# r and k of the tenth chunk on turned by a DMA in 2-byte halves, and softmax work ahead of weight conversion

## The chip, the cores and the metric

One NeuronCore of a Trainium2 chip runs the whole kernel. The metric is the device time of one launch in microseconds (us), the median of several runs. The engines named below are PE (TensorE: matmuls and transposes, with PEld for its weight loads), DVE (VectorE), ACT (ScalarE), POOL (GpSimd) and SP (SyncE, which here only issues DMAs). Each engine works through its own instructions strictly in the order in which the program puts them; semaphores hold an instruction until what it needs is there.

## The reference

A linear attention with a decaying state (RWKV-5) feeds a feed-forward block with a SoLU and a layer norm:

```
for t in range(S):                       # B=4, H=8, S=768, D=48
    cur = einsum('bhd,bhe->bhde', u * k[t], v[t])
    y[t] = einsum('bhd,bhde->bhe', r[t], state + cur)
    state = w * state + einsum('bhd,bhe->bhde', k[t], v[t])
x = y as (3072, 384)
h = x @ w_in                             # 384 -> 1024
solu = h * softmax(h)
ln = (solu - mean) / sqrt(var + 1e-6) * g_ln
out = ln @ w_out                         # 1024 -> 384
```

The weights of the feed-forward block arrive as 8-byte floats and are turned into 4-byte ones on the chip. All other data is float32.

## The kernel before

The 3072 rows are cut into 24 **units** of 128 rows (4 batches times 6 chunks of 128 steps), numbered 0 to 23 with the batch as the fast index. A diff calls a unit's chunk by that number too: "the tenth chunk on" are units 9 to 23.

For one unit the attention does the following. `turn_r` and `turn_k` (L692, L699) transpose r and k on PE, four 128x128 transposes each through PSUM (`tr_ps`, `tk_ps`), so that the head dimension lies on the partitions; DVE multiplies the turned r by a table of inverse powers of w (`fore`) while it copies it out of PSUM (`rT`, L697), and ACT copies the turned k out (`kT`, L707). k was multiplied by its powers of w before (`decay_k`, POOL, `kp`). `weigh` and `sum_own` make each row's own term, `diagonal` (ACT, L690) lays it on a diagonal matrix `AT`. `scores` (PE, `at`, L720) makes the products of k and r, which DVE copies into `AT` behind a mask (L723). `finish` (PE) makes y (`y_ps`, L748) and the state's update (`kv_ps`, L766, not for the last chunk of a batch), ACT copies y out as `xT` (L760), DVE and POOL update the state.

The feed-forward part: `ffn_in` (PE, `h_ps`, L783) with an exponential on ACT behind it (L786), `unit` (L789) with a reciprocal and the product `solu` on DVE (L793, L795), a shift and a square on ACT (L797, L798) and two small POOL instructions for the deviation (L799, L801). `h_ps` has one buffer: the next `ffn_in` can start only when L795 has read it. `halve_ln` (L807) has ACT split the 4-byte words of `solu` into two planes of 2-byte halves (L814) and SP issue a transposing DMA of these (L816). `join_ln` (L819) has DVE weave the turned halves into words again, `lnT` (L822). `ffn_out` (PE, `o_ps`, L830) multiplies by w_out, ACT scales by the deviation (L833), SP stores.

The main loop (L841) is a software pipeline written out by hand; what it calls is the order on every engine. In **iteration i** stand, among others: loads for units i+5 and i+3; `turn_r` and `turn_k` of unit i+2; `decay_k` and `weigh` of unit i+3; `scores` of unit i+1 and `finish` of unit i; `ffn_in` and `unit` of unit j = i-2; `halve_ln` of unit i-5, `join_ln` of i-6, `ffn_out` of unit l = i-7. So iterations 2 to 6 have `ffn_in` but no `ffn_out` ("early"), 7 to 23 have all, 24 to 30 drain. Iterations -2 to 5 also convert the 14 weight pieces, w_in's six first: `convert_a` (ACT, L518), `convert_b` (DVE, L531 and L533), `convert_c` (POOL, L541) and for w_out's eight also `convert_d` (DVE, L548). Iterations 7 to 20 load each piece again for a range check (`check_words`, L559, L561).

The tiles for raw weights, for `halves` and for `turned` come from one ring of six buffers (tag "raw"). A new tile takes the buffer whose last reader stands furthest back among the free ones in program order, and its first writer waits for that reader.

Of the kernel before, what the change touches and what calls it, by code (L numbers as in the profile page):

```python
# [399 lines left out]
def direct_path(  # L400
# [26 lines left out]
    nc = tc.nc  # L427
# [10 lines left out]
    LA, LO = 2, 5  # L438
# [174 lines left out]

    kdec = const.tile([128, HP, 128], F32, name="kdec")

    def turn_table():
        kd_ps = psM.tile([128, HP, 128], F32, tag="m", name="kd_ps")
        for a in range(HP):
            nc.tensor.transpose(kd_ps[:, a, :], back[:, a, :], ident)
        nc.scalar.copy(out=kdec, in_=kd_ps)  # L620
# [70 lines left out]

    def turn_r(i):  # L692
        rT = live.setdefault(i, {})["rT"] = apool.tile([128, HP, T], F32, name="rT", bufs=3)
        ps = psM.tile([128, HP, T], F32, tag="m", name="tr_ps")
        for a in range(HP):
            nc.tensor.transpose(ps[:, a, :], pair(rpads[i % NLD], a), ident)  # L696
        nc.vector.tensor_mul(rT, ps, fore)  # L697

    def turn_k(i):  # L699
        X = live[i]  # L700
        X["kT"] = apool.tile([128, HP, T], F32, name="kT")
        ps = psM.tile([128, HP, T], F32, tag="m", name="tk_ps")

        for a in range(HP):
            nc.tensor.transpose(ps[:, a, :], pair(X["kp"] if i > 0 else kpads[0], a), ident)  # L705
        if i > 0:
            nc.scalar.copy(out=X["kT"], in_=ps)  # L707
        else:
            nc.vector.tensor_mul(X["kT"], ps, back)
# [79 lines left out]
    def unit(i):  # L789
        X = live[i]  # L790
        st = small.tile([128, 8], F32, name="st", bufs=LO + 3)
        rs, tot, ss, var, rstd = (st[:, n : n + 1] for n in range(5))
        nc.vector.reciprocal(out=rs, in_=sums[:, i : i + 1])  # L793
        solu = X["solu"] = fpool.tile([128, dff], F32, name="solu", bufs=LO + 2)
        nc.vector.scalar_tensor_tensor(out=solu, in0=X["h"], scalar=rs, in1=X["e"],  # L795
                                       op0=ALU.mult, op1=ALU.mult, accum_out=tot)
        nc.scalar.activation(out=solu, in_=solu, func=ACT.Identity, scale=-float(dff), bias=tot)  # L797
        nc.scalar.activation(out=X["e"], in_=solu, func=ACT.Square, accum_out=ss)  # L798
# [7 lines left out]

    def halve_ln(i):  # L807
        X = live[i]

        halves, turned = (wpool.tile([128, dff // 2, 2], U32, tag="raw", name=name, bufs=6)  # L810
                          .bitcast(U16).rearrange("p n o -> p (n o)")
                          for name in ("halves", "turned"))
        halves = halves.rearrange("p (o n) -> p o n", o=2)
        nc.scalar.copy(out=halves, in_=X["solu"].bitcast(U16).rearrange("p (n o) -> p o n", o=2))  # L814
        X["turned"] = turned.rearrange("p (o f t) -> p o f t", o=2, f=KF)
        nc.sync.dma_start(out=X["turned"].rearrange("p o f t -> p (o f) t"),  # L816
                          in_=halves.rearrange("p o n -> p (o n)"), transpose=True)

    def join_ln(i):  # L819
        X = live[i]  # L820
        lnT = X["lnT"] = fpool.tile([128, KF, 128], F32, name="lnT")
        nc.vector.tensor_copy(out=lnT.bitcast(U16).rearrange("p f (t o) -> p o f t", o=2),  # L822
                              in_=X["turned"])
# [17 lines left out]
    for i in range(-2, N + LA + LO):  # L841
# [10 lines left out]
        before, now = now, [todo.pop(0) for _ in range(conversions.get(i, 0))]  # L852
        if i == -2:
            turn_r(0)
            turn_k(0)
            turn_table()
# [8 lines left out]
        if i == LA:  # L865
            nc.vector.tensor_single_scalar(out=minus_g, in_=g_sb, scalar=-1.0, op=ALU.mult)
# [19 lines left out]
        for p in now[: 1 if i >= LA else 2]:  # L886
# [4 lines left out]
        if 1 <= i and i + 3 < N:  # L891
            weigh(i + 3, nc.gpsimd)
        if i == 10:
# [7 lines left out]
        if 0 <= l + 1 < N:  # L901
            join_ln(l + 1)
        if not early:
# [9 lines left out]
        elif i >= LA:  # L913
            unit(j)
# [6 lines left out]
        if i == 1:  # L921
            sum_own(3)
        if early and 0 <= i:
            diagonal(i + 2)
        for p in now[1:] if i >= LA else []:
            convert_b(p)
            convert_c(p)
# [43 lines left out]
```

## Time and profile before

| | |
|---|---|
| time, median of 3 runs (lowest to highest) | 370.79 us (370.27 to 370.82) |
| the profiled execution's own time | 370.75 us |
| its span, first to last instruction | 368.8 us |
| granted PE clock, mean | 0.999 |
| busy share of the span: PE, PEld, DVE, ACT, POOL | 95%, 58%, 50%, 64%, 40% |
| first `ffn_in` of an early iteration | 27.27 us |
| first `ffn_in` of an iteration with `ffn_out` (7) | 77.50 us |
| last matmul group starts | 358.37 us |

A row of a timeline reads: start in us, length in us, engine, line of the kernel, operation, what is written <- what is read, shapes, how many instructions were merged, and in brackets how long the engine stood idle before it and whose end released it. PE matmuls are pipelined and their ends modelled, so starts are compared rather than lengths. The profiled execution's own time lies 2.0 us above its span and 0.04 us under the median, so a change of the span is taken as a change of the time.

### The profile page before, as it was taken

What the parts mean: (1) busy time and instruction counts of PE and PEld (TensorE: products, weight loads), DVE (VectorE), ACT (ScalarE), POOL (GpSimd) and SP (SyncE); (2) the same over time, 40 slices, a digit from 0 to 9 for tenths busy, and PEclk for the clock granted to TensorE, in tenths of its full rate; (3) what the DMA queues carried; (4) which work ended last, traced back from release to release, by engine and by line L of the source; (5) the groups of instructions that cost most, each with busy time, mean ns of one, the idle gap of its engine ahead of it and who ended that gap; (6) DMA issues with size and microseconds to landing.
All of it is one profiled execution on the core that took longest, in us unless ns stands there. A gap on an engine that the chain in (4) does not pass through costs nothing.

```text
span 368.8 us, 8576 instructions
## 1 busy us (share of the span) xinstructions
PE 349.7 (95%) x3527; PEld 214.2 (58%) x3527; DVE 185.9 (50%) x333; ACT 234.2 (64%) x455; POOL 145.8 (40%) x181
## 2 busy tenths in 40 slices
PE   3789999889999999999999999999999999999994
PEld 2475566557566565565664675665655565555552
DVE  7797886784563853653553534535524323133220
ACT  3865879869756676577477477666765644556410
POOL 3889766744551442533624615515420000222000
PEclk9999999999999999999999999999999999999999
DMA  8999993784964854954836746545333033312731
GB/s 172 257 234 250 212 207 47 121 161 93 186 143 87 174 116 89 181 111 93 173 78 123 148 87 140 127 83 121 88 59 78 24 79 58 74 46 59 156 78 52
DMA packets 133533, 44.88 MB, mean 122 GB/s; under 512 B 126701, under 2 KB 129902, under 8 KB 133486
## 3 DMA queue, kind: packets, MB, share of 16 engines
q1 hardware_dynamic: 133342, 44.06, 57.4%
q8 instruction: 29, 0.48, 0.6%
q10 hardware_dynamic: 144, 0.20, 0.3%
q14 instruction: 18, 0.15, 0.1%
HBM read 26.94 MB, written 4.72 MB: 86 GB/s over the span
## 4 chain that ended last, share of the span: by engine, by line
PE 78%; DVE 10%; POOL 5%; issue 3%; ACT 2%; DMA 1%; POOLq 0%; DVEq 0%; ACTq 0%
PE o_ps L830 34%; PE h_ps L783 27%; PE y_ps L748 8%; PE at L720 4%; PE tr_ps L696 2%; DVE solu L795 2%; PE tk_ps L705 2%; DVE w_out_sb L548 2%; PE kv_ps L766 1%; DVE ma L533 1%; DVE rT L697 1%; POOL ma L541 1%; DVE AT L723 1%; ACT solu L797 1%; ACT e L798 1%
## 5 line engine op out<-in xcount | busy, mean ns | idle before, releaser
L783 PE MATMUL h_ps<-w_in_sb,xT 128*128 128x512 f32 x288 | 128.4, 595 | 5.0 <-DVE solu L795 3.9
L830 PE MATMUL o_ps<-w_out_sb,lnT 128*128 128x384 f32 x384 | 127.2, 486 | 0.0
L830 PEld LDWEIGHTS o_ps<-w_out_sb,lnT 128*128 128x128 f32 x384 | 72.9, 190 | 54.7 <-issue 9.1
L783 PEld LDWEIGHTS h_ps<-w_in_sb,xT 128*128 128x128 f32 x288 | 52.9, 190 | 64.1 <-issue 59.0
L799 POOL TENSOR_SCALAR st<-st 128x1 f32<-128x1 f32 x24 | 9.0, 375 | 149.4 <-ACT e L798 149.4
L690 ACT ACTIVATE AT<-ident,own 128x128 f32<-128x128 f32 x192 | 58.5, 390 | 5.4 <-DVE own L684 5.4
L723 DVE COPY_PREDICATED AT<-later,at 128x512 f32<-128x512 uint32 x48 | 32.8, 736 | 53.6 <-PE at L720 53.6
L786 ACT ACTIVATE e<-h_ps 128x1024 f32<-128x1024 f32 x24 | 24.6, 1023 | 44.4 <-PE h_ps L783 44.4
L822 DVE COPY lnT<-turned 128x2048 uint16<-128x2048 uint16 x24 | 37.2, 1550 | 20.6 <-DMA turned<-halves 13.3
L814 ACT COPY halves<-solu 128x2048 uint16<-128x2048 uint16 x24 | 45.5, 1894 | 0.0
L793 DVE RECIPROCAL st<-sums 128x1 f32<-128x1 f32 x24 | 3.8, 160 | 64.5 <-ACT e L786 64.5
L797 ACT ACTIVATE solu<-solu,st 128x1024 f32<-128x1024 f32 x24 | 27.4, 1142 | 13.0 <-DVE solu L795 13.0
L673 POOL TENSOR_TENSOR kp<-kpad,kdec 128x512 f32<-128x512 f32 x24 | 30.6, 1277 | 7.4 <-ACT kdec L620 6.3
L795 DVE SCALAR_TENSOR_TENSOR solu<-h_ps,st,e 128x1024 f32<-128x1024 f32 x24 | 30.8, 1284 | 2.1
L679 POOL TENSOR_TENSOR rku<-kpad,u_bc 128x384 f32<-128x384 f32 x23 | 30.8, 1341 | 0.0
L760 ACT COPY xT<-y_ps 128x384 f32<-128x384 f32 x24 | 11.4, 475 | 30.2 <-PE y_ps L748 30.2
L680 POOL TENSOR_TENSOR rku<-rku,rpad 128x384 f32<-128x384 f32 x23 | 27.8, 1209 | 1.8
L720 PE MATMUL at<-rT,kT 48*64 48x128 f32 (+1 forms) x768 | 27.9, 265 | 0.0
L720 PEld LDWEIGHTS at<-rT,kT 48*64 48x64 f32 x768 | 21.8, 139 | 10.4 <-issue 9.7
L773 POOL TENSOR_TENSOR state<-state,pw 64x192 f32<-64x192 f32 x32 | 17.0, 530 | 26.3 <-DVE state L772 25.1
L748 PE MATMUL y_ps<-AT,vt 128*32 128x128 f32 x768 | 26.3, 279 | 0.0
L798 ACT ACTIVATE e<-solu 128x1024 f32<-128x1024 f32 x24 | 25.4, 1057 | 0.8
(77 smaller groups left out, 315.6 us busy)
## 6 DMA issues: line engine op xcount, KB each, us to landing
raw<-in_moe_w_in_dram SPq DMA_DIRECT2D x12, 512.0 KB, 5.8
raw<-in_moe_w_out_dram SPq DMA_DIRECT2D x16, 384.0 KB, 4.8
kpad<-in_k_dram SPq DMA_DIRECT2D x24, 192.0 KB, 4.5
rpad<-in_r_dram SPq DMA_DIRECT2D x24, 192.0 KB, 4.6
vt<-in_v_dram SPq DMA_DIRECT2D x24, 192.0 KB, 4.5
out_dram<-o SPq DMA_DIRECT2D x24, 192.0 KB, 2.1
turned<-halves SPq DMA_TRANSPOSE x24, 4.3
u_bc<-in_u_dram ACTq DMA_DIRECT2D x1, 192.0 KB, 3.6
```

Source lines behind the costliest of these rows:

```text
L673: nc.gpsimd.tensor_mul(X["kp"].rearrange("p h d -> p (h d)"), kpads[i % NLD].rearrange("p h d -> p (h d)"), kdec.rearrange("p a d -> p (a ...
L679: engine.tensor_mul(rku, kpads[i % NLD][:, :, 0:D], u_bc)
L690: nc.scalar.activation(out=AT[:, h, :], in_=ident, func=ACT.Copy, scale=X["own"][:, h])
L720: nc.tensor.matmul(pss[q][ts(c, P), a, c * P :], X["kT"][rows, a, ts(c, P)], X["rT"][rows, a, c * P :], start=True, stop=True)
L723: nc.vector.copy_predicated(A4[:, :, q, :], later.to_broadcast([128, HP, T]), pss[q])
L748: nc.tensor.matmul(y_ps[32 * g : 32 * g + 32, j, :], lhsT, rhs, start=(g not in opened), stop=stop, skip_group_check=True)
L783: nc.tensor.matmul(h_ps[:, ts(n, NX)], X["xT"][:, j, :], w_in_sb[:, j, ts(n, NX)], start=(j == 0), stop=(j == KD - 1))
L795: nc.vector.scalar_tensor_tensor(out=solu, in0=X["h"], scalar=rs, in1=X["e"], op0=ALU.mult, op1=ALU.mult, accum_out=tot)
L797: nc.scalar.activation(out=solu, in_=solu, func=ACT.Identity, scale=-float(dff), bias=tot)
L814: nc.scalar.copy(out=halves, in_=X["solu"].bitcast(U16).rearrange("p (n o) -> p o n", o=2))
L822: nc.vector.tensor_copy(out=lnT.bitcast(U16).rearrange("p f (t o) -> p o f t", o=2), in_=X["turned"])
L830: nc.tensor.matmul(o_ps, X["lnT"][:, f, :], w_out_sb[:, f, :], start=(f == 0), stop=(f == KF - 1))
```

## The change

Units 0 to 8 are turned on PE as before. From unit 9 on (`FIRST`), r is multiplied by its powers before it is turned (`decay_r`, POOL, with the table `rdec`, which is turned once on PE in iteration 1). `halve_rk` in iteration i splits unit i+3: ACT splits `kp` (L861), DVE splits `rp` (L862), both into one tile of 2048 halves per partition, and SP issues one transposing DMA of it. `join_rk` in iteration i+1 has DVE weave the turned halves into the tile `rk` (two halves `rT` and `kT`; three buffers, where `kT` had two). The eight PE transposes, the DVE product and the ACT copy of these units are gone.

In the early iterations `unit` now stands right behind `turn_r`, ahead of the conversions; `convert_b` goes to the end of the iteration for both pieces, `convert_c` to the start of the next, `convert_d` to that one's end. `minus_g` is made in iteration 1. In all iterations the two small POOL instructions of a unit (`deviation`) stand one iteration later. `solu` has five buffers, not seven.

```diff
-    LA, LO = 2, 5
+    LA, LO, FIRST = 2, 5, 9
...
+    def decay_r(i):
+        X = live[i]
+        X["rp"] = apool.tile([128, H, P], F32, name="rp")
+        nc.gpsimd.tensor_mul(X["rp"].rearrange("p h d -> p (h d)"),
+                             rpads[i % NLD].rearrange("p h d -> p (h d)"),
+                             rdec.rearrange("p a d -> p (a d)"))
...
-        nc.gpsimd.tensor_scalar(out=var, in0=ss, scalar1=1.0 / dff, scalar2=1e-6 * dff ** 2,
-                                op0=ALU.mult, op1=ALU.add)
-        nc.gpsimd.tensor_tensor(out=rstd, in0=var, in1=neg_half, op=ALU.pow)
-        X["rstd"] = rstd
+        X["st"] = ss, var, rstd
+
+    def deviation(i):
+        ss, var, rstd = live[i]["st"]
+        live[i]["rstd"] = rstd
...
+    def turn(both):
+        turned = halves()
+        nc.sync.dma_start(out=turned.rearrange("p (n t) -> p n t", t=128), in_=both,
+                          transpose=True)
+        return turned.rearrange("p (o n t) -> p o n t", o=2, t=128)
+
+    def join(words, turned):
+        nc.vector.tensor_copy(out=words.bitcast(U16).rearrange("p n (t o) -> p o n t", o=2),
+                              in_=turned)
...
+    def halve_rk(i):
+        if i < FIRST:
+            return
+        X = live[i]
+        both = halves()
+        parts = both.rearrange("p (o e n) -> p o e n", o=2, e=2)
+        nc.scalar.copy(out=parts[:, :, 1], in_=split(X["kp"].rearrange("p h d -> p (h d)")))
+        nc.vector.tensor_copy(out=parts[:, :, 0], in_=split(X["rp"].rearrange("p h d -> p (h d)")))
+        X["turned"] = turn(both)
+
+    def join_rk(i):
+        X = factors(i)
+        join(X["rk"].rearrange("p e a t -> p (e a) t"), X["turned"])
...
+        for p in before:
+            if pieces[p][2] is not None:
+                convert_c(p)
...
-        for p in before:
-            convert_d(p)
-        if i >= LA:
-            for p in now[:1]:
-                convert_b(p)
         if -2 < i and i + 2 < N:
-            turn_r(i + 2)
+            if i + 2 < FIRST:
+                turn_r(i + 2)
+            else:
+                join_rk(i + 2)
+            if early and i >= LA:
+                unit(j)
             if i < 0 or i >= LA:
                 sum_own(i + 2)
-            turn_k(i + 2)
+            if i + 2 < FIRST:
+                turn_k(i + 2)
...
+            if i + 3 >= FIRST:
+                decay_r(i + 3)
...
+        if 0 <= j - 1 < N:
+            deviation(j - 1)
...
+        if i + 3 < N:
+            halve_rk(i + 3)
...
-        elif i >= LA:
-            unit(j)
...
+            turn_table(fore, rdec)
...
+        if i >= LA:
+            for p in before:
+                convert_d(p)
+            for p in now:
+                convert_b(p)
```

On PE, between iterations 8 and 9, stood the end of unit 8 (`y_ps`, `kv_ps`), the turning of unit 11 and the feed-forward products of units 7 and 2:

```order
L748 MATMUL y_ps_1407<-rT_1062,state0_164 32x128 x12
L748 MATMUL y_ps_1407<-AT_1167,vt2_96 32x128 x16
L766 MATMUL kv_ps_1438<-vt2_96,kp_947 32x48 x16
L696 MATMUL tr_ps_1463<-ident_151,rpad1_85 128x128 x4
L705 MATMUL tk_ps_1472<-ident_151,kp_1335 128x128 x4
L783 MATMUL h_ps_1494<-w_in_sb_104,xT_1293 128x512 x6
L830 MATMUL o_ps_1520<-w_out_sb_105,lnT_1349 128x384 x8
```

The same place on PE in the changed kernel:

```order
L762 MATMUL y_ps_1400<-rk_1057,state0_164 32x128 x12
L762 MATMUL y_ps_1400<-AT_1168,vt2_96 32x128 x16
L780 MATMUL kv_ps_1431<-vt2_96,kp_945 32x48 x16
L797 MATMUL h_ps_1484<-w_in_sb_104,xT_1291 128x512 x6
L874 MATMUL o_ps_1508<-w_out_sb_105,lnT_1339 128x384 x8
```

The two groups of four transposes are gone, and `ffn_in` follows `finish` directly.

On ACT, in iterations 6 and 7, stood the exponential of unit 4, the split of unit 1, the shift and square of unit 4, unit 6's `xT`, the diagonal of unit 8, and then iteration 7 up to its exponential (unit 5):

```order
L786 ACTIVATE e_1058,sums_206<-h_ps_1051 128x1024 [waits PE_49]
L707 COPY kT_1071<-tk_ps_1072 128x512 [waits PE_49]
L814 COPY halves_1083<-solu_701 128x2048
L797 ACTIVATE solu_1091<-solu_1091,st_1089 128x1024 [waits DVE_49]
L798 ACTIVATE e_1058,st_1089<-solu_1091 128x1024 [waits Activation_49]
L760 COPY xT_1144<-y_ps_1115 128x384 [waits PE_49]
L690 ACTIVATE AT_1167<-ident_151,own_1069 128x128 x8
L707 COPY kT_1188<-tk_ps_1189 128x512 [waits PE_49]
L814 COPY halves_1202<-solu_821 128x2048
L786 ACTIVATE e_1215,sums_206<-h_ps_1208 128x1024 [waits PE_49]
```

The same stretch on ACT in the changed kernel (`halves_1093` is the first tile of r and k, unit 9; `halves_1203` the second, unit 10; DMAHW5 is the semaphore of unit 9's transposing DMA):

```order
L800 ACTIVATE e_1053,sums_207<-h_ps_1046 128x1024 [waits PE_49]
L811 ACTIVATE solu_1066<-solu_1066,st_1064 128x1024 [waits DVE_49]
L812 ACTIVATE e_1053,st_1064<-solu_1066 128x1024 [waits Activation_49]
L721 COPY rk_1057<-tk_ps_1072 128x512 [waits PE_49]
L847 COPY halves_1087<-solu_681 128x2048
L861 COPY halves_1093<-kp_1078 128x2x512 [waits Pool_49]
L774 COPY xT_1145<-y_ps_1116 128x384 [waits PE_49]
L699 ACTIVATE AT_1168<-ident_151,own_1070 128x128 [waits DVE_49]
L699 ACTIVATE AT_1168<-ident_151,own_1070 128x128 x7
L847 COPY halves_1197<-solu_800 128x2048 [waits DMAHW0_49,DVE_49]
L861 COPY halves_1203<-kp_1186 128x2x512 [waits DVE_49,DMAHW5_49,Activation_49,Pool_49]
L800 ACTIVATE e_1215,sums_207<-h_ps_1208 128x1024 [waits PE_49]
```

The shift and square moved ahead of unit 1's split; the splits of k are new, and the one of unit 10 waits for unit 9's DMA, with iteration 7's exponential behind it.

On DVE, at the start of iteration 7, stood unit 9's product, its own term, `lnT` of unit 1 and the product `solu` of unit 5:

```order
L697 TENSOR_TENSOR rT_1179<-tr_ps_1180,tab_172 128x512 [waits PE_49]
L684 TENSOR_REDUCE own_1186<-rku_1080 128x8 [waits Pool_49]
L822 COPY lnT_1206<-turned_1084 128x2x1024 [waits DMAHW4_49]
L793 RECIPROCAL st_1226<-sums_206 128x1 [waits Activation_49]
L795 SCALAR_TENSOR_TENSOR solu_1228,st_1226<-h_ps_1208,st_1226,e_1215 128x1024 [waits DVE_49,PE_49]
```

The same place on DVE in the changed kernel:

```order
L841 COPY rk_1182<-halves_1096 128x2x1024 [waits DMAHW5_49]
L693 TENSOR_REDUCE own_1184<-rku_1082 128x8 [waits Pool_49]
L841 COPY lnT_1201<-halves_1089 128x2x1024 [waits DMAHW4_49]
L862 COPY halves_1203<-rp_1188 128x2x512 [waits DVE_49,Activation_49,Pool_49]
L807 RECIPROCAL st_1226<-sums_207 128x1 [waits Activation_49]
L809 SCALAR_TENSOR_TENSOR solu_1228,st_1226<-h_ps_1208,st_1226,e_1215 128x1024 [waits DVE_49,PE_49]
```

Where a product waited for PE stands a copy that waits for unit 9's DMA, and one more copy stands ahead of `solu`.

More of the change, by code (lines that the diff above doesn't have):

```diff
@@ L815, in halve_ln @@
-        X["turned"] = turned.rearrange("p (o f t) -> p o f t", o=2, f=KF)
-        nc.sync.dma_start(out=X["turned"].rearrange("p o f t -> p (o f) t"),
-                          in_=halves.rearrange("p o n -> p (o n)"), transpose=True)
+        both = halves()
+        nc.scalar.copy(out=both.rearrange("p (o n) -> p o n", o=2), in_=split(X["solu"]))
+        X["turned"] = turn(both)
     def join_ln(i):
         X = live[i]
-        lnT = X["lnT"] = fpool.tile([128, KF, 128], F32, name="lnT")
@@ L855, in direct_path @@
             turn_k(0)
[L856 removed]
+            turn_table(back, kdec)
             weigh(0, nc.vector)
```

44 lines of the change are left out of this document (24 added, 20 removed).

## The prediction

> **What bounds the kernel now.** I read the page first, then the chain of waits, then the timeline of PE where the chain leaves PE. The page's first part gives busy times and shares, its fourth the chain that ended last:
>
> ```profile
> span 368.8 us, 8576 instructions
> ...
> PE 349.7 (95%) x3527; PEld 214.2 (58%) x3527; DVE 185.9 (50%) x333; ACT 234.2 (64%) x455; POOL 145.8 (40%) x181
> ...
> PE 78%; DVE 10%; POOL 5%; issue 3%; ACT 2%; DMA 1%; POOLq 0%; DVEq 0%; ACTq 0%
> ```
>
> PE is busy 95% and carries 78% of the chain. An average hides stages, so the chain in order of time (start, length, what) comes next, around the start of iteration 8 and at two later places:
>
> ```profile
> 91.10 0.59 PE tr_ps L696 x4
> 91.69 0.44 PE tk_ps L705 x4
> 92.13 5.15 PE h_ps L783 x12
> ...
> 264.47 5.15 PE h_ps L783 x12
> ...
> 278.50 5.15 PE h_ps L783 x12
> ...
> 291.50 5.35 PE h_ps L783 x12
> ```
>
> From 77.5 us on the chain never leaves PE: (264.47-92.13)/12 = 14.36 us for each of twelve iterations, with the eight transposes of one unit inside. What is taken from PE there shortens the run, as long as nothing else then arrives late. Before 77.5 us it is otherwise. This is the timeline of PE, `ffn_in` of iterations 4, 5, 6, 7 and 8, and the transposes ahead of iteration 7's:
>
> ```profile
> 45.81 5.39 PE L783 MATMUL h_ps<-w_in_sb,xT 128*128 128x512 f32 x12 [0.70 <-DVE solu L795]
> 55.26 5.39 PE L783 MATMUL h_ps<-w_in_sb,xT 128*128 128x512 f32 x12 [0.16 <-PE kv_ps L766]
> 65.89 5.39 PE L783 MATMUL h_ps<-w_in_sb,xT 128*128 128x512 f32 x12 [1.33 <-DVE solu L795]
> 75.11 0.66 PE L696 MATMUL tr_ps<-ident,rpad 128*128 128x128 f32 x4
> 77.50 5.42 PE L783 MATMUL h_ps<-w_in_sb,xT 128*128 128x512 f32 x12 [1.30 <-DVE solu L795]
> 91.96 5.32 PE L783 MATMUL h_ps<-w_in_sb,xT 128*128 128x512 f32 x12
> ```
>
> PE has 9.22 us of work in an early iteration (65.89 to 75.11, no wait inside), but waits up to 1.33 us more for `solu`, which must free the only `h_ps`.
>
> **Part 1: the transposes from iteration 8's on.** Iterations 7 to 21 lose their eight transposes; 7's and 8's are counted in part 2, which leaves 13. The chain would price eight at 0.59+0.44 = 1.03 us, but `h_ps` is 0.20 us longer where none stand ahead of it (5.35 against 5.15). The cleaner price is from start to start on PE's timeline, with the transposes between (iteration 21) and without (22):
>
> ```profile
> 276.42 1.06 PE L748 MATMUL y_ps<-AT,vt 128*32 128x128 f32 x32
> ...
> 283.48 5.32 PE L830 MATMUL o_ps<-w_out_sb,lnT 128*128 128x384 f32 x16
> ...
> 290.44 1.06 PE L748 MATMUL y_ps<-AT,vt 128*32 128x128 f32 x32
> ...
> 296.68 5.32 PE L830 MATMUL o_ps<-w_out_sb,lnT 128*128 128x384 f32 x16
> ```
>
> 7.06 against 6.24: 0.82 us, of which 0.11 is a longer `h_ps`. Most iterations have `kv_ps` in between as well, and I take the same price there. 13 x 0.82 = **10.7 us**, and a period of 14.36-0.82 = 13.54. By the chain's price it would be 13.4.
>
> What is added in these iterations: on ACT half a split for a copy out of PSUM, on DVE a join and half a split for a product, on POOL a product like `kp`'s, on SP one more transposing DMA. None was seen at these sizes, so each is priced from the nearest row. ACT's timeline in iterations 5 and 6:
>
> ```profile
> 60.69 1.02 ACT L786 ACTIVATE e<-h_ps 128x1024 f32<-128x1024 f32 x1 [0.50 <-PE h_ps L783]
> 61.61 0.19 ACT L786 ACTIVATION_READ_ACCUMULATOR e<-h_ps 128x1 f32 x1
> 61.70 1.01 ACT L518 ACTIVATE low<-raw 128x384 uint32<-128x384 uint32 x2
> 62.60 0.58 ACT L707 COPY kT<-tk_ps 128x512 f32<-128x512 f32 x1
> 63.07 1.92 ACT L814 COPY halves<-solu 128x2048 uint16<-128x2048 uint16 x1
> 65.78 1.15 ACT L797 ACTIVATE solu<-solu,st 128x1024 f32<-128x1024 f32 x1 [0.79 <-DVE solu L795]
> 66.96 1.06 ACT L798 ACTIVATE e<-solu 128x1024 f32<-128x1024 f32 x1
> 68.01 0.46 ACT L760 COPY xT<-y_ps 128x384 f32<-128x384 f32 x1
> 68.37 2.44 ACT L690 ACTIVATE AT<-ident,own 128x128 f32<-128x128 f32 x8
> ```
>
> Half of 1.92 is 0.95 us for the split of k, less 0.58 for `kT`. DVE's timeline in iterations 5 and 6 and in iteration 14:
>
> ```profile
> 60.89 1.41 DVE L548 TENSOR_SCALAR w_out_sb<-ma,minus_g 128x384 f32<-128x384 f32 x1 [2.57 <-POOL ma L541]
> ...
> 64.26 0.15 DVE L793 RECIPROCAL st<-sums 128x1 f32<-128x1 f32 x1
> 64.45 1.28 DVE L795 SCALAR_TENSOR_TENSOR solu<-h_ps,st,e 128x1024 f32<-128x1024 f32 x1
> ...
> 74.03 2.05 DVE L822 COPY lnT<-turned 128x2048 uint16<-128x2048 uint16 x1
> ...
> 178.73 0.54 DVE L684 TENSOR_REDUCE own<-rku 128x8 f32<-128x384 f32 x1
> 179.50 0.55 DVE L561 TENSOR_REDUCE least<-mag 128x1 f32<-128x384 f32 x1 [0.24 <-ACT mag L559]
> 179.97 1.42 DVE L822 COPY lnT<-turned 128x2048 uint16<-128x2048 uint16 x1
> ```
>
> A join is 1.4 us (2.05 beside POOL), half a split 0.7 (up to 1.28, the full-width pass over as many elements). Now, of 14.4 us, and alone at the end:
>
> ```profile
> 92.10:106.50 14.40, 14.40 (x158) 8.89 (x157) 7.45 (x12) 9.63 (x19) 5.91 (x8) 1.00 0.75 153
> 291.50:304.69 13.19, 13.19 (x117) 7.55 (x117) 4.03 (x7) 6.27 (x8) 0.74 (x2) 1.00 0.25 56
> ```
>
> Columns of this table by windows: the stretch, its length, busy time of PE, PEld, DVE, ACT and POOL, then clock, DMA share and GB/s. ACT goes from 9.6 to 10.0, DVE from 7.5 to 9.0, POOL from 5.9 to 7.2, all under 13.54, and each in a stretch where it idles today. The transposing DMA:
>
> ```profile
> L816 SPq DMA_TRANSPOSE turned<-halves x24: 1605/1926/3370, 65.0 to 350.6; - x24
> ...
> DMA to landing us min/median/max: 4.2/4.3/6.5
> ```
>
> In the steady state, counted from `ffn_in`'s start, DVE does the state's update, a join, `own`, `least`, another join and the split of r, done near 5.7 if the state's update takes the first 1.0; SP issues then, and the halves land near 10.0. They are wanted when the next iteration's first join can start, about 13.54+1.0. That is 4.5 us of cover; I cost the path at nothing.
>
> **Part 2: up to iteration 8's `ffn_in`.** With `unit` ahead of the conversions, `solu` no longer stands behind L548, which waited 2.57 us for POOL's `ma`. It is freed by `ffn_in`'s start +5.43 (55.26 to 60.69) to the exponential, +1.2 (with its accumulator), +0.19 to `solu`'s start, +1.33 to its end: 8.15, under 9.22. So PE sets the pace, if ACT is free. Iteration 4 starts at 45.81-0.70 = 45.1, 5 at 54.3, 6 at 63.55, 7 at 72.8. ACT in iteration 5, by starts: exponential 59.75, conversions (in the shadow of `solu`), shift 62.45, square 63.6, `kT` 64.7, split 65.15, `xT` 66.95, diagonals 67.3 to 69.7. Iteration 6's exponential starts there, 0.7 late; its `solu` ends at 69.7+2.72 = 72.4, still before 72.8. Four waits gone, and iteration 7's transposes too.
>
> Then a new wait appears. ACT in iteration 6: shift 72.4, square 73.6, `kT` 74.65, split of unit 1 75.1 to 77.0, split of k of unit 9 to 78.0. SP issues the first transposing DMA at 77.0, is busy with it 1.9, issues unit 9's at 78.9; +4.3 lands at **83.2**. DVE stands at `join_rk` of unit 9 meanwhile, with `own`, a join, the split of unit 10's r and then `solu` of unit 5 queued behind it: 83.2+1.4+0.5+1.4+0.7 = 87.2, +0.19+1.33 and a semaphore of 0.1 gives **88.85** for iteration 8's `ffn_in`. ACT waits too: its split of unit 10's k takes unit 9's buffer and so that DMA, 83.3 to 84.2, then unit 5's exponential to 85.4, earlier than DVE. PE alone would be ready at 72.8+13.54 = 86.3, so 2.5 us of the early gain go back. Iteration 8 starts 91.96-88.85 = **3.1 us** earlier. In iteration 8 unit 10's DMA lands at 87.3+4.3 = 91.6, and with the splits and unit 6's exponential behind it on ACT and the two joins on DVE `solu` ends at some 98.5, before PE's 88.85+13.54 = 102.4: the wait doesn't recur. From iteration 22 on all stands as before. The once turned `rdec` costs four transposes (0.6, as `tr_ps` above) in iteration 1 ahead of a wait of `ffn_in` of 0.99 us for DVE on the same timeline; nothing. `deviation` one iteration later is wanted five iterations later; nothing.
>
> ```profile
> 27.27 5.42 PE L783 MATMUL h_ps<-w_in_sb,xT 128*128 128x512 f32 x12 [0.99 <-DVE ma L533]
> ```
>
> **Sum.** 10.7+3.1-0.1 (iteration 8's own longer `h_ps`) = 13.7. The profiled execution took 370.75, 0.04 under the median: 370.8-13.7 = **357.1 us**. Bounds: a DMA as slow as 6.5, or joins of 2.05, move iteration 8 by 2 (359.1); the chain's price of transposes by 2.7 the other way (354.4).
>
> **A rule against the change.** The row says that sixteen 128x128 blocks of halves land 4.3 us after their issue. The Trainium skill (VectorE: DVE Perf Modes, The three transpose paths and Rules for kernel authors) gives 1309 ns for one such block by DMA against 390 ns on TensorE, and advises TensorE where PSUM will do. Taken block by block that would be an estimated 21 us for a unit; the trace has a fifth of it. By that rule the slow rival below would come true, at some 510 us.
>
> **Rivals.**
> - *No wait ahead of iteration 8.* If the DMA of unit 9 or the queue on DVE is 2.5 us faster than I add up, PE starts iteration 8 at 86.3 and the run takes 354.6. For: my ACT order leaves little slack either way. Against: two DMAs in a row on one SP queue. Chance 0.20 (354.2 to 356).
> - *The early part gains nothing.* Iteration 7 stays at 77.5, because ACT, DMA or POOL takes the place of DVE; the wait of 16.05 us to iteration 8 then ends at 93.6, 1.6 late: 10.7-1.6-0.1 = 9.0, 361.8. For: ACT is 0.7 late in iteration 6 already. Chance 0.12 (359.5 to 363).
> - *The DMA engines fill up.* 0.75 of 14.40 is 10.8 us of transfers; a transposing DMA with a store was 0.25 of 13.19, 3.3 us. Together 14.1, over 13.54 in the six iterations with w_in's pieces: 6 x 0.56 = 3.4 back, 360.5. Against: windows before 55 us moved 209 GB/s and more. Chance 0.06.
> - *Slower: the halves come too late in every iteration.* Split, DMA, join, `own`, `least`, join and next split form a ring: landing time + 4.6. It passes 14.36 from a landing of 9.8 us, and eats the 3 us of part 2 from 10.0. At 11 the run loses 13 x 1.24 - 3.0 = 13 and takes 384. The longest landing in the trace is 6.5. Chance 0.05.
> - *It does not do what it says*: the transposes stay, or go where PE waits anyway. The order on PE and the unbroken chain speak against it; 370.8, chance 0.02.
>
> **How the numbers follow.** The forecast, 356 to 359.5, has 0.55. The range runs from the first rival to the second, 354.2 to 362.0, and leaves out some 0.13. A measurement tells about 0.2% from no change: faster 0.93, same 0.02, slower 0.05.
>
> **What would show it.** After: a period of about 13.5 on PE's chain from iteration 8 to 20; no wait for `solu` at the starts of iterations 4 to 6 and a `ffn_in` of iteration 7 near 73; one wait of 2 to 3 us for `solu` ahead of iteration 8, behind a DVE that waited for a transposing DMA; landings near 4.3. Wrong if the period stays near 14.4, if waits for that DMA recur, or if PE waits ahead of every `ffn_in`.

## The result and the profile after

| | before | changed |
|---|---|---|
| time, median (lowest to highest) | 370.73 us (370.27 to 370.82) | 359.43 us (357.99 to 360.58) |
| the profiled execution's own time | 370.75 us | 357.99 us |
| its span | 368.8 us | 356.3 us |

The ratio of the times is 0.9696, with a 95% interval of 0.9659 to 0.9733: faster by 11.3 us. The forecast was 357.1 us, in a range of 354.2 to 362.0. The execution that was profiled is the shortest of the changed kernel's four, so what the longer ones do isn't in its profile.

The page of the changed kernel, its first part and the shares of its chain:

```profile
span 356.3 us, 8402 instructions
...
PE 337.3 (95%) x3411; PEld 201.9 (57%) x3411; DVE 214.1 (60%) x348; ACT 242.5 (68%) x456; POOL 180.6 (51%) x196
...
PE 80%; DVE 6%; ACT 5%; issue 4%; POOL 2%; DMA 1%; POOLq 0%; DVEq 0%; ACTq 0%
```

PE lost 12.4 us of work and 116 matmuls, and its share is 95% as before: every other engine is busier in a shorter span, and PE is still the bound. Its timeline at the `ffn_in` of iterations 4, 7, 8 and 9:

```profile
45.10 5.42 PE L797 MATMUL h_ps<-w_in_sb,xT 128*128 128x512 f32 x12
...
72.85 5.42 PE L797 MATMUL h_ps<-w_in_sb,xT 128*128 128x512 f32 x12
...
89.14 5.42 PE L797 MATMUL h_ps<-w_in_sb,xT 128*128 128x512 f32 x12 [2.69 <-DVE solu L809]
102.67 5.42 PE L797 MATMUL h_ps<-w_in_sb,xT 128*128 128x512 f32 x12
```

H7 and H8 are short for the starts of iteration 7's and 8's `ffn_in` from here on. H7 came from 77.50 to 72.85 us; then 2.69 us of that gain are waited away, and H8 is 2.82 us earlier than the 91.96 of before. From there an iteration takes 102.67-89.14 = 13.53 us, where it took 14.36.

The chain of waits, in order of time, shows what PE waited for:

```profile
79.01 4.97 DMA halves<-halves
84.01 0.07 DVE rk L841
...
85.25 0.55 DVE own L693
85.80 1.24 DVE lnT L841
87.04 0.57 DVE halves L862
87.61 0.08 DVE st L807
87.79 1.30 DVE solu L809 x2
89.14 5.42 PE h_ps L797 x12
```

Unit 9's transposing DMA lands at 83.98, and behind its join stand `own`, the other join, unit 10's split and then `solu`, for which PE waits. In the steady part no such wait is left. There the table by windows reads, for one whole iteration (columns as in the prediction):

```profile
197.50:211.03 13.53, 13.53 (x149) 8.02 (x149) 9.14 (x12) 10.07 (x20) 8.50 (x8) 1.00 0.78 166
```

PE is busy for all of 13.53 us, DVE for 9.1, ACT for 10.1, POOL for 8.5.

### The profile page after: what moved, and what is told of

It is laid out like the page before. It is cut to its first block, busy times and chain, and to the rows that moved or that the text cites. A ratio compares the mean times of both kernels' runs of the same rounds, so it can differ in the third digit from the quotient of the medians.

```text
span 356.3 us, 8402 instructions
## 1 busy us (share of the span) xinstructions
PE 337.3 (95%) x3411; PEld 201.9 (57%) x3411; DVE 214.1 (60%) x348; ACT 242.5 (68%) x456; POOL 180.6 (51%) x196
## 4 chain that ended last, share of the span: by engine, by line
PE 80%; DVE 6%; ACT 5%; issue 4%; POOL 2%; DMA 1%; POOLq 0%; DVEq 0%; ACTq 0%
PE o_ps L874 33%; PE h_ps L797 31%; PE y_ps L762 8%; PE at L734 5%; ACT AT L699 1%; DVE solu L809 1%; DMA halves<-halves 1%; PE kv_ps L780 1%; DVE part L531 1%; DVE AT L737 1%; ACT solu L811 1%; ACT e L812 1%; ACT halves L847 1%; DVE ma L533 1%; POOL rku L689 1%
## 5 line engine op out<-in xcount | busy, mean ns | idle before, releaser
L797 PE MATMUL h_ps<-w_in_sb,xT 128*128 128x512 f32 x288 | 129.9, 600 | 3.8 <-DVE solu L809 3.2
L787 POOL TENSOR_TENSOR state<-state,pw 64x192 f32<-64x192 f32 x32 | 25.6, 801 | 65.4 <-DVE state L786 64.2
L841 DVE COPY lnT<-halves 128x2048 uint16<-128x2048 uint16 x24 | 38.2, 1592 | 20.7 <-DMA halves<-halves 13.3
L682 POOL TENSOR_TENSOR rp<-rpad,rdec 128x512 f32<-128x512 f32 x15 | 30.6, 2043 | 0.0
L841 DVE COPY rk<-halves 128x2048 uint16<-128x2048 uint16 x15 | 21.2, 1413 | 12.1 <-DMA halves<-halves 11.8
L734 PE MATMUL at<-rk 48*64 48x128 f32 (+1 forms) x768 | 27.9, 265 | 0.0
L734 PEld LDWEIGHTS at<-rk 48*64 48x64 f32 x768 | 21.8, 139 | 10.4 <-issue 9.3
L861 ACT COPY halves<-kp 128x1024 uint16<-128x1024 uint16 x15 | 15.7, 1046 | 16.4 <-POOL kp L675 13.2
L862 DVE COPY halves<-rp 128x1024 uint16<-128x1024 uint16 x15 | 20.6, 1370 | 10.1 <-POOL rp L682 10.1
L688 POOL TENSOR_TENSOR rku<-kpad,u_bc 128x384 f32<-128x384 f32 x23 | 26.4, 1147 | 0.0
```

Of the source, the lines that this page charges most:

```text
L682: nc.gpsimd.tensor_mul(X["rp"].rearrange("p h d -> p (h d)"), rpads[i % NLD].rearrange("p h d -> p (h d)"), rdec.rearrange("p a d -> p (a ...
L734: nc.tensor.matmul(pss[q][ts(c, P), a, c * P :], X["kT"][rows, a, ts(c, P)], X["rT"][rows, a, c * P :], start=True, stop=True)
L797: nc.tensor.matmul(h_ps[:, ts(n, NX)], X["xT"][:, j, :], w_in_sb[:, j, ts(n, NX)], start=(j == 0), stop=(j == KD - 1))
L841: nc.vector.tensor_copy(out=words.bitcast(U16).rearrange("p n (t o) -> p o n t", o=2), in_=turned)
```

## The experiments

Times of before on the chips of these runs lay between 370.2 and 371.5 us.

### What each part gives alone

**e1, the order alone.**

```diff
-    LA, LO, FIRST = 2, 5, 9
+    LA, LO, FIRST = 2, 5, 24
```

> The new order of the early iterations alone: r and k of all 24 units turned by TensorE, as before (the first unit turned by the DMA is set to 24). The prediction's parts are separate: without the transposing DMA H7 comes about one set of transposes after the 72.85 us of the changed kernel, near 73.7, there is no wait on unit 1's join ahead of iteration 8, so H8 stands near 88 (91.96 before), and from there the period is 14.36 us again: 370.8 - 3.8 = about 367.0 us. Rival, that the early order gains nothing by itself: 370.8 us. Rival, that all of the gain is of the order: 359.5 us.

Measured: 368.66 us (368.37 to 369.94), ratio 0.9956 (0.9941 to 0.9971). That is 1.8 us, half of what was expected. PE's timeline of e1, the turns ahead of H7, H7 itself and H8:

```profile
72.63 0.66 PE L711 MATMUL tr_ps<-ident,rpad 128*128 128x128 f32 x4
75.10 0.63 PE L719 MATMUL tk_ps<-ident,kp 128*128 128x128 f32 x4 [1.81 <-ACT rk L721]
75.56 5.32 PE L797 MATMUL h_ps<-w_in_sb,xT 128*128 128x512 f32 x12
...
89.93 5.32 PE L797 MATMUL h_ps<-w_in_sb,xT 128*128 128x512 f32 x12
```

The early iterations run as in the changed kernel, but ahead of H7 stand the turns of unit 9, and with them a wait of 1.81 us that the kernel before did not have: the turn of k (`tk_ps`) waits for ACT's copy of the last turned k. H8 is 2.03 us earlier than before, and the period is 14.36 again.

**e9, the DMA alone**, with the order of before in the early iterations.

```diff
-        for p in before:
-            if pieces[p][2] is not None:
-                convert_c(p)
...
-            if early and i >= LA:
-                unit(j)
...
+        elif i >= LA:
+            unit(j)
+            deviation(j)
```

> The DMA alone: r and k turned by it from unit 9 on, with the order of unit and weight pieces in iterations 2 to 7 as it was before. Theory (the order gave some 3 us, the DMA the rest): H7 stays near 77, since TensorE waited for VectorE's solu there before (1.3 us, H7 = 77.5) and the turns of unit 9 that are taken away lay ahead of that wait; H8 = 91 to 92 with no large wait, since unit 9's halves have more time; from there the period is 13.53: 359.8 to 361 us. Rival (the wait ahead of iteration 8 is of the DMA and comes on top): H8 = 93 to 94, 362 to 363 us. Rival (the order is worth nothing beside the DMA): 357.5 to 358.5 us.

Measured: 361.63 us (360.55 to 363.41), ratio 0.9773 (0.9743 to 0.9803); the profiled execution took 360.84. PE's timeline of e9, H7 and H8:

```profile
78.37 5.39 PE L797 MATMUL h_ps<-w_in_sb,xT 128*128 128x512 f32 x12 [3.09 <-DVE solu L809]
91.88 5.42 PE L797 MATMUL h_ps<-w_in_sb,xT 128*128 128x512 f32 x12
```

H8 is where it was before (91.96). The eight transposes ahead of H7 are gone, but PE only waits longer there for `solu`, 3.09 us in place of 1.30, and the split of r stands ahead of `solu` on DVE. What is left is the steady part: from H8 to the last output's end it is 261.92 us in e9 and in the changed kernel alike, and 272.6 in before and in e1.

**e2, the DMA from unit 16 on** (`LA, LO, FIRST = 2, 5, 16`).

> The DMA turns r and k from unit 16 on. Each unit it turns takes eight transposes (0.82 us by the rows of before) off TensorE: the eight units 16 to 23 give 6.6 us, so 367.0 - 6.6 = about 360.4 us, with the DMA first issued long after the early part, so no wait of TensorE on its first join. If the chain's own price of the transposes held (1.03 us an iteration), 358.8 us. If the slope is 0, 367 us.

Measured: 362.79 us (362.05 to 364.16), ratio 0.9791 (0.9766 to 0.9815), 5.9 less than e1. PE's timeline of e2 at the `ffn_in` of iterations 13 to 15, where the turns stop:

```profile
163.26 5.32 PE L797 MATMUL h_ps<-w_in_sb,xT 128*128 128x512 f32 x12
176.69 5.42 PE L797 MATMUL h_ps<-w_in_sb,xT 128*128 128x512 f32 x12
190.23 5.42 PE L797 MATMUL h_ps<-w_in_sb,xT 128*128 128x512 f32 x12
```

In the profiles the stretch from iteration 13's `ffn_in` to the last one is 156.81 us in e2 and 163.43 in e1: 6.62 us for eight units, 0.83 each. The time expected was too low mostly because its start, e1's time, was.

### The wait ahead of iteration 8

**e3, the DMA from unit 10 on** (`LA, LO, FIRST = 2, 5, 10`).

> The DMA turns r and k from unit 10 on, one unit later. Theory (the wait of 2.7 us ahead of iteration 8 comes of unit 9's first transposing DMA, which is issued behind unit 1's and joined ahead of unit 1's join): H7 one set of transposes later (about 73.7), no such wait, H8 near 87.3, so about 1.8 us ahead of the changed kernel: a span near 354.5 us where the changed kernel's was 356.3. Rival (the wait is not the first rk tile's but comes of the queue of transposing DMAs getting started): it stands ahead of iteration 9 instead, and the time is the changed kernel's or 0.8 us above it.

Measured: 359.76 us (357.96 to 360.26), ratio 0.9688 (0.9668 to 0.9709): the changed kernel's time, so the expectation failed. But the rival's reason is not the one either. PE's timeline of e3 around H7:

```profile
75.57 0.63 PE L719 MATMUL tk_ps<-ident,kp 128*128 128x128 f32 x4 [1.80 <-ACT rk L721]
76.03 7.01 PE L797 MATMUL h_ps<-w_in_sb,xT 128*128 128x512 f32 x12
...
91.16 1.13 PE L797 MATMUL h_ps<-w_in_sb,xT 128*128 128x512 f32 x2
```

The wait for the DMA is gone, none stands ahead of iteration 9 either, and the one of e1 has come in its place, 1.80 us. Behind it the same twelve matmuls take 7.01 us and not 5.42. The table by windows of e3 shows why (the third number from the end is the granted clock):

```profile
76.00:77.00 1.00, 1.00 (x4) 0.49 (x3) 0.97 (x3) 1.00 (x1) 0.92 (x2) 0.57 0.00 0
77.00:78.00 1.00, 1.00 (x2) 0.46 (x2) 0.97 (x3) 1.00 (x4) 0.93 (x1) 0.50 0.00 0
78.00:79.00 1.00, 1.00 (x2) 0.34 (x1) 0.39 (x1) 1.00 (x5) 1.00 (x2) 0.50 0.56 113
79.00:80.00 1.00, 1.00 (x3) 0.42 (x2) 0.00 (x0) 1.00 (x5) 1.00 (x2) 0.72 1.14 215
```

PE ran at half clock for 3.4 us after the wait and lost 1.6 us by it (7.01-5.42).

**e7, e3 with one copy moved from ACT to DVE.**

```diff
-        if i > 0:
+        if i == 8:
+            nc.vector.tensor_copy(out=X["kT"], in_=ps)
+        elif i > 0:
             nc.scalar.copy(out=X["kT"], in_=ps)
```

> The kernel of e3 (the DMA from unit 10 on), with unit 8's turned k copied out of PSUM by VectorE and not by ScalarE. In e3 TensorE waited 1.8 us in iteration 7 at the second turn (tk_ps) for that copy, which stood on ScalarE behind unit 4's e, solu and square, and its granted clock then fell to 0.5 for some 3 us, which cost 1.6 us more. Theory (the four PSUM buffers of these tiles go round, and the copy holds one): with the copy on VectorE ahead of solu the wait falls under 0.5 us, H7 = 74 to 74.5, the clock stays at 1, H8 = 87.5 to 88.2, time 356.3 to 357.0 us. Rival (tk_ps waits for something else): H7 76, time 358 to 360 us.

Measured: 356.16 us (356.02 to 356.32), ratio 0.9606 (0.9588 to 0.9624). PE's timeline of e7, the turn of k, H7 and H8:

```profile
73.30 0.63 PE L719 MATMUL tk_ps<-ident,kp 128*128 128x128 f32 x4
73.76 5.32 PE L799 MATMUL h_ps<-w_in_sb,xT 128*128 128x512 f32 x12
87.20 5.42 PE L799 MATMUL h_ps<-w_in_sb,xT 128*128 128x512 f32 x12
```

No wait is left at either place, and the clock stays at 1. So both steps of e3's account hold: the new order leaves unit 8's k in one of the four PSUM buffers until ACT has done unit 4's shift and square, and a turn in iteration 7 needs that buffer. This also settles the missing 1.8 us of e1. The changed kernel escapes the wait because its iteration 7 turns nothing on PE.

**e4, unit 9's halves ahead of unit 1's.**

```diff
+        if i == 6:
+            halve_rk(i + 3)
         if 0 <= l + 2 < N:
             halve_ln(l + 2)
...
-        if i + 3 < N:
+        if i + 3 < N and i != 6:
             halve_rk(i + 3)
```

> In iteration 6 alone, unit 9's halves and their DMA are issued ahead of unit 1's, so that the first join of r and k, which VectorE meets first, has its data first. Theory (the wait ahead of iteration 8 is this order of two DMAs and nothing else): unit 9's halves land near 80.5 instead of 83.4, VectorE's wait at that join falls from 5.6 to about 2.5 us, H8 = 86.4, the wait is gone, and the span is about 353.6 us (2.7 less than the changed kernel's). Rival (what ends last is unit 1's join or ScalarE's chain): H8 stays at 89.1 and the time does too.

Measured: 355.94 us (355.82 to 356.50), ratio 0.9609 (0.9596 to 0.9623). This is the lowest median here, with e7 close behind. It lies 2.7 us under the median of the changed kernel's ten executions (358.67, with e8 and e12), and 2.0 us of that are H8. Its rows are H8 on PE's timeline and unit 9's join on DVE's:

```profile
87.17 5.39 PE L797 MATMUL h_ps<-w_in_sb,xT 128*128 128x512 f32 x12 [0.63 <-DVE solu L809]
...
80.79 2.18 DVE L841 COPY rk<-halves 128x2048 uint16<-128x2048 uint16 x1 [2.32 <-DMA halves<-halves]
```

The wait fell from 2.69 to 0.63 us by the order of two DMAs. It isn't nil as expected: the halves landed about when expected, at 80.77, but the join takes 2.18 us here, beside POOL, and not 1.4, and the 0.8 us more are enough for the 0.63.

**e10, e4 with unit 10's halves behind iteration 7's `solu`**, to take the rest.

```diff
-        if i + 3 < N and i != 6:
+        if i + 3 < N and i not in (6, 7):
             halve_rk(i + 3)
...
                 unit(j)
+            if i == 7:
+                halve_rk(i + 3)
```

> The kernel of e4, and in iteration 7 the halves of unit 10 behind the SOLU product of that iteration and not ahead of it. Theory: of the 0.63 us that TensorE still waited ahead of iteration 8 in e4, VectorE's split of r (0.67) is the last part, so the wait is gone, H8 = 86.5 to 86.6, and the span is 0.6 us under the 354.2 of e4: about 355.3 us. Rival (unit 10's halves, later by some 1.5 us, move the wait to iteration 9): 356 us or above.

Measured: 356.94 us (356.10 to 357.54), ratio 0.9622 (0.9609 to 0.9635): 1 us slower than e4. PE's timeline of e10, H8 and the start of iteration 11's `ffn_in`:

```profile
87.58 5.39 PE L797 MATMUL h_ps<-w_in_sb,xT 128*128 128x512 f32 x12 [0.21 <-DVE solu L809]
...
128.99 5.42 PE L797 MATMUL h_ps<-w_in_sb,xT 128*128 128x512 f32 x12 [0.77 <-DVE solu L809]
```

The wait ahead of iteration 8 is down to 0.21, and 0.77 us appear three iterations on: the rival's way, only later. Another 0.84 us of the profiled execution stand at its start, where iteration 2 begins that much later than e4's. The joins of r and k run 1.3 us behind e4's in iteration 8 (95.11 against 93.80) and 3.0 in iteration 10 (119.09 against 116.06), where a check that runs once stands on DVE as well.

**e11, e10 with the DMA from unit 8 on.**

```diff
-    LA, LO, FIRST = 2, 5, 9
+    LA, LO, FIRST = 2, 5, 8
...
-        if i == 6:
+        if i in (5, 6):
             halve_rk(i + 3)
...
-        if i + 3 < N and i not in (6, 7):
+        if i + 3 < N and i not in (5, 6, 7):
```

> The kernel of e10 with the DMA from unit 8 on, its halves issued in iteration 5 ahead of unit 0's. One more set of eight transposes off TensorE: if ScalarE and VectorE, which are full in iterations 5 to 7, and the landing allow it, H7 = 72.1, H8 = 85.7 and 354.5 us. Rival (ScalarE's and VectorE's chains, 1 us and 2 us longer by unit 8's split and join, set H7 and H8): a wait of 1 to 3 us ahead of H7 or H8, and 355.5 to 358 us.

Measured: 359.26 us (359.11 to 359.43), ratio 0.9696 (0.9681 to 0.9711): the rival's wait, but above its 355.5 to 358. H7 on PE's timeline of e11:

```profile
75.08 7.09 PE L797 MATMUL h_ps<-w_in_sb,xT 128*128 128x512 f32 x12 [2.72 <-DVE solu L809]
```

A wait of 2.72 us has moved to iteration 7, and again half a clock stands behind it, 7.09 us for 5.42, which the rival had no price for.

### How much cover the DMA has

**e5 and e6, two and three DMAs in a row.** Both are e4 with the transposing DMA of r and k issued two or three times into the same tile, from unit 12 on.

```diff
-    def turn(both):
+    def turn(both, times=1):
...
         turned = halves()
-        nc.sync.dma_start(out=turned.rearrange("p (n t) -> p n t", t=128), in_=both,
-                          transpose=True)
+        for _ in range(times):
+            nc.sync.dma_start(out=turned.rearrange("p (n t) -> p n t", t=128), in_=both,
+                              transpose=True)
...
-        X["turned"] = turn(both)
+        X["turned"] = turn(both, 2 if i >= 12 else 1)
```

In e6 the 2 is a 3.

> The kernel of e4, with the transposing DMA of r and k issued twice into the same tile from unit 12 on, so that its landing takes about twice as long (4.4 us to between 8.8 and 10). Theory (the DMA has cover): in the steady part its halves land about 155.6 us and VectorE joins them at 157.7, and the SOLU product that stands behind the join on VectorE ends at 152.4, 6.4 us ahead of the h_ps at 158.8 that needs its buffer; so a landing later by 4.4 to 5.6 us makes VectorE wait 2.3 to 3.5 us at each join and TensorE not at all: 355.9 us, within 0.5. Rival (the transposing DMA is at its limit, on its queue or on the 16 DMA engines): what exceeds 2.1 us is paid in each of 12 iterations, 28 us and more: 384 us.

> The same with three DMAs from unit 12 on: a landing of 13 to 15 us, 8.8 to 10.6 later. By the cover of the steady part (2.1 us to the join and 6.4 more to the h_ps) that is 0.3 to 2.1 us too late in each of 12 iterations: between 359 and 381 us, with waits of TensorE for VectorE's solu. Were the cover larger, 355.9 us; were it only the 2.1 us, 436 us.

Measured: e5 374.53 us (370.39 to 375.90), ratio 1.0092 (1.0064 to 1.0120); e6 426.08 us (three executions from 424.33 to 426.52, and one of 431.02), ratio 1.146 (1.1426 to 1.1495). Both expectations failed. DVE's timeline of e5, the split of r, the next join and the next split:

```profile
187.05 0.68 DVE L863 COPY halves<-rp 128x1024 uint16<-128x1024 uint16 x1
...
199.91 1.32 DVE L842 COPY rk<-halves 128x2048 uint16<-128x2048 uint16 x1 [7.94 <-DMA halves<-halves]
...
203.27 0.68 DVE L863 COPY halves<-rp 128x1024 uint16<-128x1024 uint16 x1
```

The same on DVE's timeline of e6, from a join to the next one:

```profile
207.94 1.36 DVE L842 COPY rk<-halves 128x2048 uint16<-128x2048 uint16 x1 [12.10 <-DMA halves<-halves]
211.30 0.68 DVE L863 COPY halves<-rp 128x1024 uint16<-128x1024 uint16 x1
227.88 1.35 DVE L842 COPY rk<-halves 128x2048 uint16<-128x2048 uint16 x1 [12.56 <-DMA halves<-halves]
```

From the end of a split to the join it is 12.2 us in the one and 15.9 in the other, and from there to the end of the next split 4.0 in both. The parts add up to one turn of the ring, 16.2 and 19.9 us; over the steady part the turns average 15.4 and 19.5, with 11.4 and 15.5 for split to join. A ring carries each late arrival into the next iteration, so what a turn has over the period of 13.53 us is paid in every iteration: 1.9 and 5.9 us. The two averages lie 4.1 us apart, for one DMA more. By that a turn with a single DMA would be some 11.3 us, and its **cover**, the period less one turn, some 2.2 us; this is an estimate from the two turns. The rows of the changed kernel agree with it. DVE's split of r and the join behind it there:

```profile
149.52 1.48 DVE L862 COPY halves<-rp 128x1024 uint16<-128x1024 uint16 x1 [1.13 <-POOL rp L682]
...
157.72 1.35 DVE L841 COPY rk<-halves 128x2048 uint16<-128x2048 uint16 x1
```

The DMA between them was issued at 151.1 us and landed 4.3 us later, at 155.4, which is 2.3 us ahead of the join. Two things keep the cover that small. In the turn of e5 above SP is still busy with the transposing DMA of `solu`'s halves when the split ends, and issues the one of r and k only at 190.2, after 2.4 of the 12.2 us; its two DMAs then land 5.3 and 4.3 us after their issue, the second issued when the first has landed. And in the changed kernel the part on DVE, from the start of the join to the end of the split, takes 6.8 us (144.18 to 151.00) and not 4.0, because POOL holds it up. The rival's reason is seen in no more than those 2.4 us of SP's queue: the transposing DMAs themselves land after 4.4 us in the median of e5 and 4.3 of e6, as in the changed kernel. So the first 2.1 us of the expectations were nearly the whole cover. Their mistake was to count the distance to PE's need of one iteration on top, as if it came anew each time.

### Why the times of the changed kernel lie apart

**e8 and e12, the changed kernel again**, unaltered.

> The changed kernel once more, unaltered, since its four times lie 2.6 us apart (357.99 to 360.58) and those of e4 0.7 us. Theory: the wait of 2.7 us ahead of iteration 8 lets TensorE's clock fall for some us afterwards in some executions, worth 1 to 2.5 us; an execution above 359 us shows a stretch of granted clock below 1 just behind that wait, one near 358 does not, and all else is the same within 0.3 us. Rival: the difference lies in the loads at the start or in the last store.

> The changed kernel unaltered a third time, to see one of its longer executions in a profile (two of them were profiled at 357.99 and 358.18 us, and both had TensorE's clock at 1 behind the wait of 2.7 us ahead of iteration 8; the ones that weren't profiled reach 360.6). Theory: an execution above 359 us has the same H8 within 0.3 us and the same wait, and an h_ps behind it of 7.0 to 7.1 us in place of 5.42, with the granted clock near 0.5, as e11 had behind its wait of 2.7 us: 1.6 us. Rival: the difference stands at the start (H2 later than 28.5) or at the end. An execution near 358 us tells nothing more.

Measured: 358.74 us (357.61 to 359.39), ratio 0.9675 (0.9645 to 0.9705), and 357.96 us in two executions. All three that were profiled are among the short ones (357.99, 358.18 and 357.87 us), with H8 at 89.14, 89.38 and 88.86 and an `ffn_in` of 5.42 us there, so none shows what a long one does. The ten times form two groups, five from 357.61 to 358.18 and five from 359.15 to 360.58, whose means are 1.7 us apart. That is the price of one stretch of half clock in e11 (7.09-5.42 = 1.67) behind the same length of wait, and e4 and e7, whose waits there are 0.63 us and none, spread over 0.7 and 0.3 us. It fits, but it is argued, not shown. The mean granted clock on record for each execution points the same way and doesn't settle it: four of the five long ones have 0.992 or 0.993, but the fifth (359.30) has 0.997, and the short ones lie between 0.983 and 0.998. Nor is the rival of a late start excluded: in the profiles of all these kernels H2, the start of iteration 2's `ffn_in`, lies between 27.12 and 28.71 us.

## Why the prediction was right, point by point

**Part 1 held to 0.1 us.** It forecast 10.7 us less in the 13 iterations and a period of 13.54. From H8 to the last output the profile has 272.6 and 261.9: 10.7; the period is 13.53. e2 gives 0.83 us a unit against 0.82; the chain's price of 1.03 would have given 8.2 for eight units and 13.4 for thirteen.

**Work added beside PE at no cost: right in effect, off in sizes.** The groups by line of the changed kernel, busy time and mean ns behind the bar:

```profile
L682 POOL TENSOR_TENSOR rp<-rpad,rdec 128x512 f32<-128x512 f32 x15 | 30.6, 2043 | 0.0
L841 DVE COPY rk<-halves 128x2048 uint16<-128x2048 uint16 x15 | 21.2, 1413 | 12.1 <-DMA halves<-halves 11.8
L862 DVE COPY halves<-rp 128x1024 uint16<-128x1024 uint16 x15 | 20.6, 1370 | 10.1 <-POOL rp L682 10.1
L861 ACT COPY halves<-kp 128x1024 uint16<-128x1024 uint16 x15 | 15.7, 1046 | 16.4 <-POOL kp L675 13.2 <-DMA halves<-halves 1.7 <-DVE rk L841 1.5
```

The join was forecast at 1.4 and is 1.41; ACT's split 0.95, is 1.05. DVE's split was 0.7 and is 1.37, POOL's product was priced like `kp` and takes 2.04. Neither reaches PE in the steady part, where 2.3 us of cover were left. In e4 a join beside POOL does reach it, ahead of iteration 8.

**The cover and the ring: right in form, too large in size.** The prediction has the ring and costs its path at nothing, and no wait recurs. But its cover of 4.5 us is 2.3 in the changed kernel's rows and about 2.2 by e5 and e6. It had the split done 5.7 us after `ffn_in`'s start and it is 7.7 (143.27 to 151.00), since DVE's rows are longer beside POOL. Its formula, landing plus 4.6, puts the 4.6 where e5 and e6 have 4.0, and has no term for the up to 2.4 us until SP issues. With a cover of 4.5 the second DMA of e5 would have been nearly free; it cost 18.6 us (374.53-355.94), two stretches of half clock included. The slow rival is nearer than it was priced: at 15.5 us from split to join the kernel takes 426 us. It did not come true since the 39 transposing DMAs landed after 4.4 us in the median (4.3 to 6.8). A DMA engine share of 1.06 in one iteration (102.67 to 116.20 us) cost PE nothing there, so the rival of full DMA engines did not come true either.

**Part 2 named the right wait and its releaser.** H4 45.1 and H7 72.8 were forecast, and 45.10 and 72.85 measured; a wait of 2.5 (2.69) and H8 88.85 (89.14). Two sizes inside were off and nearly cancel: the second DMA landed 0.8 us later (4.97 on the chain and not 4.3), and DVE's queue behind it was 0.5 shorter. The prediction's reason, two DMAs in a row on one queue with the later one joined first, is shown by e4, where that order alone is turned round.

**What part 2 had not seen** is how its two gains hang together. It adds up four waits that go by the order and iteration 7's transposes that go by the DMA, and never asks about the PSUM buffers of the turns. The order by itself brings H8 2.03 us forward (e1), the DMA by itself 0.08 (e9), both 2.82. Without the order PE waits at H7 for `solu` where the transposes stood, and without the DMA it waits for a PSUM buffer. That the changed kernel was spared this second wait is luck as far as the prediction goes. The DMA isn't the only way around it either: e7, with the DMA from unit 10 on, turns unit 9 on PE, moves one copy, and has H8 at 87.20. The rival that the early part gains nothing, at 361.8, lies near e9's time of 361.63, but not by its way: it had iteration 8 start at 93.6, and e9 starts it at 91.88.

**What is left of the difference.** The profiled execution took 357.99, 0.9 us over the forecast: 0.3 is H8, 1.0 stands behind the last output, and 0.3 came off again between the span and the execution's own time (2.0 us before, 1.7 after). ACT's last row in before and in the changed kernel:

```profile
363.97 0.58 ACT L833 ACTIVATE o<-o_ps,st 128x384 f32<-128x384 f32 x1 [4.90 <-PEq L939]
```

```profile
350.48 0.58 ACT L877 ACTIVATE o<-o_ps,st 128x384 f32<-128x384 f32 x1 [4.90 <-PEq L994]
```

From its end to the span's it is 4.25 us before and 5.24 after. That was 4.0 in e1 and 4.3 in e2, and 5.1 to 5.5 in all kernels that turn from unit 8, 9 or 10 on, with the same one store in it; why stays open. The rest of the median's 2.3 us is the spread of the times (e8 and e12), whose cause isn't shown.

## What to carry to other kernels

When a transfer takes over work of the busiest engine, write down the ring that it closes (last writer, the wait until its queue issues it, transfer, first reader, and what stands between that reader and the next writer), for its cover is the period less one turn and not the slack that PE has in a single pass. At the place where the steady loop begins, the order in which two transfers are issued should be that in which they are joined: that alone brought H8 2.0 us forward (e4). And a part of a change is to be tried alone before its share is believed, since a wait that one part opens may be closed by the other.

## What the runs showed of the hardware

**Half a clock behind a short wait.** After PE had waited 1.80 us (e3), 2.72 us (e11), or 2.34 and 2.65 us (two places of e5), its granted clock was 0.50 for a while, 3.4 us long in e3 and e11, and the `ffn_in` behind took 7.0 to 8.5 us and not 5.42. The same was seen behind all ten waits of 2.9 to 9.1 us in e6. Behind ten waits of 0.6 to 1.78 us (e4, e5, e6) it was not, nor behind 1.81 us in e1, 2.6 to 2.7 us in the changed kernel's three profiles and 3.09 us in e9. The Trainium skill (TensorE: Matmul & The Clock Gate, Part 1: The HAM clock gate) states a half-rate state, and a window of 3413 ns that runs freely and measures how busy TensorE was. The length of the stretch and the half agree with it, and a window that runs freely would explain why waits of one length differ in effect. The page wants an idle window of some 3.4 us for it; here waits of little more than half of that were enough, and the measurement decides.

**DVE and POOL hold each other up.** POOL's product of r and the row behind it, on POOL's timeline of the changed kernel between the `ffn_in` of iterations 12 and 13, and beside them DVE's join of `lnT` and its split of r, on DVE's timeline:

```profile
147.17 2.32 POOL L682 TENSOR_TENSOR rp<-rpad,rdec 128x512 f32<-128x512 f32 x1
149.44 1.00 POOL L688 TENSOR_TENSOR rku<-kpad,u_bc 128x384 f32<-128x384 f32 x1
```

```profile
146.48 1.92 DVE L841 COPY lnT<-halves 128x2048 uint16<-128x2048 uint16 x1
149.52 1.48 DVE L862 COPY halves<-rp 128x1024 uint16<-128x1024 uint16 x1 [1.13 <-POOL rp L682]
```

In e5, where the two engines work at different times, the product takes 1.27 us and the split 0.68. Here the product starts at 147.17, DVE's copy ends at 148.40, and 1.27 from about there is the product's end at 149.49; the split starts at 149.52, POOL's row ends at 150.44, and 0.6 from there is the split's end at 151.00. To within 0.2 us each waits until the other is through and then runs at its own speed. So the Trainium skill has it (SBUF — State Buffer, Who interferes with whom): a pair of ports that the two share, which a DVE copy can take, locked for a whole instruction; these rows agree.
